# Pair products of a second set moved behind a stage of the chain on TensorE, and their inversion begun later

## The chip, the core and the metric

The kernel runs on one core of a Trainium2 chip. The metric is the device time of one execution, in microseconds; the time of a kernel is the median of its runs. A profile of one more execution shows where the time goes. The engines are TensorE (PE in the rows, PEld its weight loads), VectorE (DVE), ScalarE (ACT), GpSimd (POOL) and SyncE (SP), which issues most DMAs.

## The reference

A linear recurrence over 768 time steps for 4 x 8 heads, followed by a two-layer network on its outputs.

```python
for t in range(S):
    kt, vt, rt = (k[:, :, t], v[:, :, t], r[:, :, t])
    wt, at, bt = (w[:, :, t], a[:, :, t], b[:, :, t])
    y[:, :, t] = np.einsum('bhd,bhde->bhe', rt, state)
    Sa = np.einsum('bhde,bhe->bhd', state, at)
    state_decay = state * wt[:, :, None, :] - np.einsum('bhd,bhe->bhde', Sa, bt)
    state = state_decay + np.einsum('bhd,bhe->bhde', vt, kt)
...
h = x @ w_in
g = np.where(pos, h, np.where(neg, 0.0, (h + beta) ** 2 / (4.0 * beta)))
return (g @ w_out).astype(np.float32)
```

Here x is y laid out as 3072 tokens of 320, and w_in and w_out are 320 x 2048 and 2048 x 320.

## The kernel before

**Tiling.** The recurrence is cut into 24 chunks of 32 time steps; within a chunk it becomes small matmuls per head, with the inverse of a 32 x 32 triangular matrix for each head and chunk. Four chunks make a set (six sets). For a set the kernel needs the decayed rows of the inputs, the pair products of a and b (early_ab, line 208, for sets 0 and 1: 64 matmuls into one PSUM tile, line 217, copied to the tile `pairs` by ScalarE, line 221; called once for each half of the set), and the inversion (invert, line 361): `pairs` is turned on VectorE into `lw` (line 365), GpSimd sets the unit matrix (lines 367, 368), and then 31 pairs of products and subtractions follow (lines 376, 382), on VectorE for set 0 and on GpSimd for the others. adopt (line 385) turns the result into `tinv`.

**The chain** (line 517) runs a chunk in two halves of 16 heads, each in four stages: x0 (matmuls of line 532), the product with `tinv` (line 542, masks on VectorE at line 549, ScalarE copies at line 553), the state and the outputs (matmuls of lines 558 and 569, VectorE at 576 and 581), and the next state's product (lines 598, 600). The loop over chunks takes four steps for each chunk; each step runs one or two stages, loads and turns inputs (load_ti and load_cg; shift, line 323 on ScalarE; turn, lines 477, 480 and 482 on VectorE; scores, lines 498 and 510), and then calls fill. The first stage of chunk 0 is already run while set 0 is inverted; its second stage stands in the second step, its third in the third step.

**Fill** (line 928) hands out other work in six parts: columns of the two-layer network (feed; it begins only when two chunks of y have been laid out again, lines 618 to 627), one entry of the list `steps` (line 907), the conversion of the weights (wgen: ScalarE lines 764, 768 and 784, VectorE 772, GpSimd 785), and the background work (rows, ab and inv of later sets), whose pace is set by the table WINDOWS in chunks times ten: a window (a, b) for a set says when its work begins and when it must be done.

```python
            feed(1280)
            if first:
                first.pop(0)()
            due[0] += PACE
            while due[0] > 0:
                pull(wgen)
                due[0] -= 1
            background(now[0] + 10 / SLOTS * (k + 1) / 6)
```

Every engine works through its instructions in the order in which this program writes them.

Of the kernel before, what the change touches and what calls it, by code (L numbers as in the profile page):

```python
# [27 lines left out]
WINDOWS = dict(  # L28
    rows=[(0, 0), (24, 43), (46, 64), (70, 90), (106, 130)],
    ab=[(0, 0), (44.5, 55.5), (68, 84), (95, 119), (135, 159)],  # L30
    inv=[(2.1, 28), (56, 79.5), (85, 118), (121, 158), (161, 198)],
)

AHEAD = 5
# [21 lines left out]
def rwkv_moe_kernel(ctx: ExitStack, tc: tile.TileContext, r, k, v, w, a, b, w_in, w_out, ident_d, mask_d, out):  # L56
# [62 lines left out]
    def zero(x, row=0):  # L119
        z = zero_c[row : row + x.shape[0]]  # L120
        nc.scalar.copy(x, (z if len(x.shape) == 2 else z.unsqueeze(1)).broadcast_to(list(x.shape)))

    def init_cg(i, part):
        cg, pr = cgs[i], prs[i]
        if part == 0:
            return zero(cgf[i])
        if part == 2:
            return nc.gpsimd.memset(pr[:, :, :, 0:8], -1.0)
        for f in range(2):
            rows = slice(64 * f, 64 * f + D)  # L130
            nc.scalar.copy(
                cg[rows, f::2, C_G : C_G + D],
                ident[rows].unsqueeze(1).broadcast_to([D, 8, D]),
            )

    def copy_rv(s, part, c, n=1):

        x, o = ((r, O_R), (v, O_V))[part]
        nc.sync.dma_start(
            scr[s][0 : NH * 128].rearrange("(h x) e -> h x e", x=128)[:, L * c : L * (c + n), o : o + D],  # L140
            x.rearrange("b h t e -> (b h) t e")[:, 128 * s + L * c : 128 * s + L * (c + n), :],
        )
# [65 lines left out]
    def early_ab(s, half):  # L208

        ps = psum()  # L210
        for c in (2 * half, 2 * half + 1):
            for h in range(NH):
                p, f = h // 2, h % 2
                q, n = 2 * f + p % 2, 4 * p + c
                rows = slice(64 * f, 64 * f + D)
                at = 256 * (c % 2) + 32 * (p // 2)
                nc.tensor.matmul(
                    ps[32 * q : 32 * q + 32, at : at + 32],
                    lhsT=turned[s][0][rows, n, :], rhs=turned[s][1][rows, n, :], start=True, stop=True,
                )  # L220
        nc.scalar.copy(pairs_f[:, 512 * half : 512 * half + 512], ps)

    def early_store(s, c):

        nc.sync.dma_start(scr4[s][c, :, :, 80:240], early_out[s][c::4])
# [668 lines left out]
    i = 0  # L894
# [9 lines left out]
    owed, idle = [0], [True]  # L904
    now = [0]
    due = [0]
    steps = [[lambda half=half: early_ab(1, half)] for half in range(2)] + [[lambda: init_cg(2, 2)]] + [[lambda i=i, c=c: copy_rv(0, i, c)] for c in (2, 3) for i in range(2)]
    steps += [[] for _ in range(7)] + [[lambda c=c: early_store(1, c)] for c in range(4)] + [[] for _ in range(8)]
    steps += [[lambda i=i: copy_rv(1, i, 0, 4)] for i in range(2)]
    first = [lambda x=x: [f() for f in x] for x in steps]  # L910

# [118 lines left out]
```

## Time and profile before

| | |
|---|---|
| median of 3 runs | 779.89 us (777.26 to 780.51) |
| the profiled execution | 778.53 us, its span 776.8 us |
| TensorE busy, mean granted clock | 672.8 us (87%), 0.916 |
| VectorE, ScalarE, GpSimd busy | 589.2, 472.4, 433.2 us |
| HBM read, written | 70.88 MB, 27.53 MB |

Times in the rows count from the span's start. A timeline row gives start, duration, engine, line, operation, tiles and shape, and in brackets the idle time of the engine before it and what ended that. "issue" is idle time in which the engine waited for nothing that the profile shows. A matmul in float32 is shown as two records, so the 64 matmuls of one early_ab are 128 records. The granted clock is a share of the full 2.4 GHz; 0.50 is 1.2 GHz.

### The profile page before, as it was taken

To read this page: it belongs to the slowest core of one execution; us is meant where nothing else is said; L and a number is where in the kernel's file an instruction comes from. 1 tells how busy PE (TensorE), PEld (TensorE's weight loads), DVE (VectorE), ACT (ScalarE), POOL (GpSimd) and SP (SyncE) were. 2 spreads that over 40 slices of the span, in tenths; PEclk is the share of its full clock that TensorE was granted. 3 is DMA by queue.
4 is the path that set the end of the run, shared out by engine and by line. 5 is a ranking of instruction groups with operands and counts; after the bars stand their busy time and mean duration, and the time that the engine had idled before them with its cause. 6 is when DMAs were issued, how large, how long until landed. Compare 5 with 4: busy or idle time off the path is not lost.

```text
span 776.8 us, 35626 instructions
## 1 busy us (share of the span) xinstructions
PE 672.8 (87%) x15360; PEld 620.9 (80%) x15360; DVE 589.2 (76%) x1361; ACT 472.4 (61%) x1016; POOL 433.2 (56%) x603
## 2 busy tenths in 40 slices
PE   4546656796889889899988999999999999999997
PEld 4445546685779778789988889999999999999997
DVE  6999998887769678897788977788777786776211
ACT  5646756775566565565666566665665665655544
POOL 1232999765336998367576486563666732322332
PEclk9865656999699999999999999999999999999999
DMA  8898996998587758684558683443424234330100
GB/s 296 210 218 174 229 204 171 221 211 182 123 183 161 171 133 172 144 191 89 124 115 173 143 171 71 109 80 62 116 47 110 54 71 108 55 89 20 36 20 18
DMA packets 207084, 102.35 MB, mean 132 GB/s; under 512 B 153688, under 2 KB 200792, under 8 KB 206928
## 3 DMA queue, kind: packets, MB, share of 16 engines
q1 hardware_dynamic: 204336, 93.36, 54.2%
q0 software_dynamic: 2432, 6.56, 3.7%
q8 instruction: 121, 1.98, 1.1%
q14 instruction: 35, 0.29, 0.1%
q10 hardware_dynamic: 160, 0.16, 0.1%
HBM read 70.88 MB, written 27.53 MB: 127 GB/s over the span
## 4 chain that ended last, share of the span: by engine, by line
PE 54%; DVE 6%; POOL 4%; DMA 3%; ACT 2%; issue 2%; SPq 2%; POOLq 0%; ACTq 0%; DVEq 0%
PE ph L650 18%; PE po L681 17%; PE p L569 4%; PE p L558 3%; PE p L598 3%; PE p L498 2%; PE p L542 2%; PE p L532 2%; PE p L349 1%; DMA X<-Y 1%; POOL lw L382 1%; POOL lw L376 1%; POOL gl L667 1%; DVE gt L663 1%; DVE wz L235 1%
## 5 line engine op out<-in xcount | busy, mean ns | idle before, releaser
L650 PE MATMUL ph<-X,w 120*128 120x256 f32 x1536 | 219.7, 296 | 6.3 <-DMA X<-Y 5.8
L667 POOL TENSOR_TENSOR gl<-gt,gh 128x512 fp32r<-128x512 f32 x95 | 121.6, 1280 | 162.3 <-ACT gh L666 155.8
L650 PEld LDWEIGHTS ph<-X,w 120*128 120x128 f32 x1536 | 198.0, 198 | 13.9 <-issue 6.0
L681 PE MATMUL po<-w,gh 128*128 128x320 f32 x768 | 136.6, 320 | 4.6 <-ACT gh L666 3.8
L663 DVE SCALAR_TENSOR_TENSOR gt<-gt,ph 128x512 f32<-128x512 f32 x95 | 65.0, 684 | 85.2 <-ACT gt L661 72.8
L681 PEld LDWEIGHTS po<-w,gh 128*128 128x128 f32 x768 | 119.5, 197 | 6.7 <-ACT gh L666 5.0
L666 ACT CAST gh<-gt 128x512 fp32r<-128x512 f32 x95 | 58.8, 619 | 91.7 <-DVE gt L663 84.8
L660 ACT ACTIVATE gt<-ph,half_c 128x512 f32<-128x512 f32 x95 | 65.3, 687 | 54.5 <-PE ph L650 53.7
L382 POOL TENSOR_TENSOR lw<-lw 128x31 f32<-128x31 f32 (+15 forms) x155 | 86.9, 561 | 8.3
L376 POOL TENSOR_TENSOR lw<-lw 128x31 f32<-128x31 f32 (+15 forms) x155 | 85.5, 551 | 8.1
L576 DVE SCALAR_TENSOR_TENSOR cg<-p,pr 40x160 f32<-40x160 f32 x184 | 59.2, 322 | 34.6 <-PE p L569 32.5
L681 PE MATMUL po<-w,gl 128*128 128x320 f32 x384 | 75.8, 320 | 9.5 <-POOL gl L667 9.5
L510 DVE TENSOR_TENSOR cg<-p,mask 32x256 f32<-32x256 f32 x192 | 80.6, 420 | 3.6
L553 ACT ACTIVATE cg<-p 32x160 f32<-32x160 f32 x192 | 56.6, 295 | 30.6 <-DVE cg L549 16.3
L681 PEld LDWEIGHTS po<-w,gl 128*128 128x128 f32 x384 | 62.3, 195 | 11.6 <-POOL gl L667 11.3
L569 PE MATMUL p<-cg 128*64 128x72 f32 (+1 forms) x1536 | 64.0, 241 | 0.0
L549 DVE SCALAR_TENSOR_TENSOR cg<-p,mask 32x128 f32<-32x128 f32 x192 | 55.3, 288 | 11.0 <-ACT cg L553 5.8
L589 POOL TENSOR_TENSOR Y<-yt,Y 128x256 fp32r<-128x256 f32 x48 | 35.7, 744 | 48.5 <-ACT Y L588 48.4
L661 ACT ACTIVATE gt<-gt 128x512 f32<-128x512 f32 x95 | 60.0, 632 | 3.0
L569 PEld LDWEIGHTS p<-cg 128*64 128x64 f32 x1536 | 58.4, 150 | 0.4 <-issue 0.4
L558 PEld LDWEIGHTS p<-cg 128*40 128x40 f32 x1472 | 36.4, 131 | 21.2 <-ACT cg L553 13.1
L558 PE MATMUL p<-cg 128*40 128x40 f32 x1472 | 42.6, 219 | 12.2 <-ACT cg L553 12.2
(105 smaller groups left out, 1085.1 us busy)
## 6 DMA issues: line engine op xcount, KB each, us to landing
ti<-scr SPq DMA_DIRECT2D x96, 200.0 KB
cg<-scr SPq DMA_DIRECT2D x96, 80.0 KB
scr<-arena SPq DMA_DIRECT2D x16, 480.0 KB
X<-Y SPq DMA_DIRECT2D x36, 160.0 KB
scr<-wide SPq DMA_DIRECT2D x8, 640.0 KB
w<-in_moe_w_out_dram SPq DMA_DIRECT2D x16, 320.0 KB
tiab<-scr SPq DMA_DIRECT2D x28, 160.0 KB
cg<-scr SPq DMA_DIRECT2D x96, 40.0 KB
```

The source lines that it names most:

```text
L376: eng.tensor_mul(t3, W3[:, 0:n, j : j + 1].broadcast_to([128, n, m]), L3[:, j + 1 :, j].unsqueeze(1).broadcast_to([128, n, m]),)
L382: eng.tensor_sub(W3[:, 0:n, j + 1 :], W3[:, 0:n, j + 1 :], t3)
L510: nc.vector.tensor_tensor(out=cg[q, f::2, C_X : C_X + 64][:, 4 * i : 4 * i + 4].rearrange("p h (j x) -> p h j x", x=32), in0=ps[quarter(f, ...
L558: nc.tensor.matmul(pst[er[h % 2], h // 2, :], lhsT=cg[:, h, C_S : C_S + D], rhs=cg[:, h, C_G : C_G + D], start=True, stop=True)
L569: nc.tensor.matmul(psv[h // 8][64 * f : 64 * f + 64, h // 2 % 4, 0:n3], lhsT=cgw[:, h * CW + C_G : h * CW + C_G + 64], rhs=cg[:, h, C_R : ...
L576: nc.vector.scalar_tensor_tensor(out=cn[er[f], f::2, C_S : C_S + D][:, halves[i]], in0=psv[i][er[f], :, 32:72], scalar=-1.0, in1=pr[er[f], ...
L650: nc.tensor.matmul(phs[k % 2][:, n * j : n * j + n], lhsT=wt[0, f // 4, wi // 2][:, wi % 2, fs], rhs=Xs[g][:, xi, :], start=i == 0, stop=i ...
L660: nc.scalar.activation(gt, ph, AF.Relu, bias=half_c, scale=0.5)
L661: nc.scalar.activation(gt, gt, AF.Square)
L663: nc.vector.scalar_tensor_tensor(out=gt, in0=gt, scalar=1.0, in1=ph, op0=ALU.min, op1=ALU.max)
L667: nc.gpsimd.tensor_sub(gl, gt, gh.bitcast(F32))
L681: nc.tensor.matmul(pos[i], lhsT=x[:, ts_], rhs=w, start=q == 0 and k == 0, stop=end)
```

## The change

Two things. In the list `steps`, of which each fill hands out six entries, the two halves of early_ab for set 1 move from the first two places (first step) to places 6 and 7 (the first two parts of the second step's fill, which stand behind the second stage of the chain). What stood behind them moves up by two places: the clearing of `pr2`, the four copies of r and v for chunks 2 and 3, the four stores of set 1 and its two copies of r and v. And the window of set 1's inversion begins at 3.4 and not at 2.1; its end stays at 28.

```diff
-    inv=[(2.1, 28), (56, 79.5), (85, 118), (121, 158), (161, 198)],
+    inv=[(3.4, 28), (56, 79.5), (85, 118), (121, 158), (161, 198)],
...
-    steps = [[lambda half=half: early_ab(1, half)] for half in range(2)] + [[lambda: init_cg(2, 2)]] + [[lambda i=i, c=c: copy_rv(0, i, c)] for c in (2, 3) for i in range(2)]
-    steps += [[] for _ in range(7)] + [[lambda c=c: early_store(1, c)] for c in range(4)] + [[] for _ in range(8)]
+    steps = [[lambda: init_cg(2, 2)]] + [[lambda i=i, c=c: copy_rv(0, i, c)] for c in (2, 3) for i in range(2)]
+    steps += [[]] + [[lambda half=half: early_ab(1, half)] for half in range(2)] + [[] for _ in range(4)] + [[lambda c=c: early_store(1, c)] for c in range(4)] + [[] for _ in range(8)]
```

TensorE around the second stage of the chain's first half chunk, before (p are PSUM tiles, cg_85 the operands of chunk 0's first half, wide_104 the turned a and b of set 1):

```order
L532 MATMUL p_759<-cg_85 32x72 x16
L217 MATMUL p_819<-wide_104 32x32 x64
L217 MATMUL p_887<-wide_104 32x32 x64
L542 MATMUL p_963<-x_760,tinv 32x72 x2
...
L498 MATMUL p_991<-cg_86,ev 32x32 x16
L498 MATMUL p_991<-pr_89,ev 32x32 x16
L558 MATMUL p_1045<-cg_85 40x40 x16
```

and now:

```order
L532 MATMUL p_759<-cg_85 32x72 x16
L542 MATMUL p_829<-x_760,tinv 32x72 x2
...
L498 MATMUL p_857<-cg_86,ev 32x32 x16
L498 MATMUL p_857<-pr_89,ev 32x32 x16
L217 MATMUL p_901<-wide_104 32x32 x64
L217 MATMUL p_968<-wide_104 32x32 x64
L558 MATMUL p_1045<-cg_85 40x40 x16
```

The 128 matmuls of line 217 moved from ahead of the second stage (L542, eight rows in all) to between the scores (L498) and the third stage (L558).

VectorE at the same place (ti_82 are the next chunk's inputs, X the weights in conversion, cg_87 the next chunk's operands):

```order
 L772 SCALAR_TENSOR_TENSOR X_93<-X_93 120x512
-L365 STREAM_TRANSPOSE lw<-pairs 128x1024
-L549 SCALAR_TENSOR_TENSOR cg_85<-p_963,mask 32x4x32 x2
-L549 SCALAR_TENSOR_TENSOR cg_85<-p_964,mask 32x4x32 x2
-L510 TENSOR_TENSOR cg_86<-p_991,mask 32x4x64 x4
+L549 SCALAR_TENSOR_TENSOR cg_85<-p_829,mask 32x4x32 x2
+L549 SCALAR_TENSOR_TENSOR cg_85<-p_830,mask 32x4x32 x2
+L510 TENSOR_TENSOR cg_86<-p_857,mask 32x4x64 x4
 L482 STREAM_TRANSPOSE pr_90<-ti_82 128x16x32
 L772 SCALAR_TENSOR_TENSOR X_92<-X_92 120x512
+L365 STREAM_TRANSPOSE lw<-pairs 128x1024
 L772 SCALAR_TENSOR_TENSOR X_93<-X_93 80x512
```

The turn of the pairs (L365) moved from ahead of the masks (L549) to between two steps of the weights' conversion, behind L482 and ahead of L576.

GpSimd where the inversion of set 1 begins (w are converted weights):

```order
+L785 ISA
+L785 TENSOR_TENSOR w_00_1036<-X_93,w_00_1036 120x512
 L367 MEMSET lw 128x1024
 L368 MEMSET lw 128x32
-L785 ISA
-L785 TENSOR_TENSOR w_00_1039<-X_93,w_00_1039 120x512
-L785 TENSOR_TENSOR w_01_1113<-X_92,w_01_1113 120x512
+L785 TENSOR_TENSOR w_01_1114<-X_92,w_01_1114 120x512
+L785 TENSOR_TENSOR w_02_1123<-X_93,w_02_1123 80x512
+L790 DMA w_02_1123<-w_02_1123 40x512 x2
 L376 TENSOR_TENSOR lw<-lw 128x31
 L382 TENSOR_TENSOR lw<-lw 128x31
```

The first product of the inversion (L376) stands behind the third weight tile (w_02) and not behind the second. On ScalarE the two copies of line 221 move behind the shift of the next chunk's inputs (L323) and stand ahead of the weights' next L764.

## Rows read from the trace of the kernel before

**Rows 1.** Table of stretches: window, its length, busy us, clock, DMA share, GB/s.

```profile
52.00:60.00 8.00, 2.43 (x135) 1.99 (x136) 7.21 (x24) 0.40 (x1) 3.29 (x7) 0.50 0.99 231
60.00:67.00 7.00, 4.33 (x233) 3.80 (x232) 6.91 (x10) 4.16 (x8) 1.11 (x2) 0.50 0.49 130
67.00:80.00 13.00, 8.70 (x236) 7.67 (x237) 11.67 (x28) 9.18 (x21) 5.88 (x8) 0.50 1.06 215
80.00:125.00 45.00, 27.06 (x804) 24.07 (x804) 39.51 (x88) 30.80 (x72) 42.53 (x60) 0.65 1.01 202
...
450.00:730.00 280.00, 279.98 (x6376) 261.98 (x6375) 205.56 (x494) 172.79 (x380) 139.52 (x192) 1.00 0.36 79
```

In rows 1 the five busy times are those of PE, PEld, DVE, ACT and POOL, each with its count of instructions.

**Rows 2.** Timeline of TensorE (first row: its weight loads), 52 to 131 us.

```profile
52.11 0.25 PEld L532 LDWEIGHTS p<-cg 128*32 128x32 f32 x8 [0.26 <-issue]
...
52.56 1.82 PE L217 MATMUL p<-wide 40*32 40x32 f32 x119
59.95 1.93 PE L217 MATMUL p<-wide 40*32 40x32 f32 x128 [5.57 <-issue]
63.40 0.34 PE L217 MATMUL p<-wide 40*32 40x32 f32 x9 [1.52 <-issue]
63.67 1.18 PE L542 MATMUL p<-x,tinv 32*32 32x72 f32 x32
64.78 0.65 PE L498 MATMUL p<-cg,ev 40*32 40x32 f32 x32
65.23 0.63 PE L498 MATMUL p<-pr,ev 40*32 40x32 f32 x32
67.58 1.54 PE L558 MATMUL p<-cg 128*40 128x40 f32 x31 [1.73 <-ACT cg L553]
...
68.99 2.16 PE L569 MATMUL p<-cg 128*64 128x72 f32 x31
...
130.14 1.20 PE L650 MATMUL ph<-X,w 120*128 120x256 f32 x4 [2.69 <-DMA X<-Y]
```

**Rows 3.** DMA queues of the whole span: packets, MB, share of 16 engines.

```profile
q8 instruction: 121, 1.98, 1.1%
```

**Rows 4.** Timeline of VectorE, 60 to 74 us.

```profile
60.10 2.01 DVE L389 STREAM_TRANSPOSE tinv<-lw 128x1024 f32<-128x1024 f32 x1
...
63.46 0.71 DVE L480 STREAM_TRANSPOSE ev<-ti 128x512 f32<-128x512 f32 x1
...
64.67 1.94 DVE L365 STREAM_TRANSPOSE lw<-pairs 128x1024 f32<-128x1024 f32 x1
...
70.51 0.71 DVE L482 STREAM_TRANSPOSE pr<-ti 128x512 f32<-128x512 f32 x1 [0.91 <-ACT ti L323]
71.14 1.34 DVE L772 SCALAR_TENSOR_TENSOR X<-X 120x512 uint32<-120x512 uint32 x2
72.51 1.33 DVE L576 SCALAR_TENSOR_TENSOR cg<-p,pr 40x160 f32<-40x160 f32 x4
```

**Rows 5.** Timeline of ScalarE, 63 to 71 us.

```profile
63.80 0.58 ACT L221 COPY pairs<-p 128x512 f32<-128x512 f32 x1 [1.58 <-PE p L217]
...
70.02 0.45 ACT L323 COPY ti<-ti 32x320 f32<-32x320 f32 x1 [0.39 <-DMA ti<-scr]
```

**Rows 6.** Waits of SP's DMA queue, 40 to 130 us: total, times, longest.

```profile
SPq L317 <- DMA scr<-in_r_dram: 10.9, 1, 10.9
```

**Rows 7.** Timeline of GpSimd, 75 to 80 us.

```profile
75.15 1.28 POOL L785 TENSOR_TENSOR w<-X,w 120x512 fp32r<-120x512 f32 x1 [1.53 <-ACT w L784]
76.39 0.68 POOL L376 TENSOR_TENSOR lw<-lw 128x31 f32<-128x31 f32 x1
...
78.43 1.26 POOL L785 TENSOR_TENSOR w<-X,w 80x512 fp32r<-80x512 f32 x1
```

**Rows 8.** Waits of all engines, 60 to 140 us: total, times, longest.

```profile
ACT X L764 <- POOL w L785: 5.8, 3, 3.5
...
DVE yt L581 <- POOL Y L589: 2.4, 2, 1.9
```

## Prediction

> **What bounds the kernel now.** I read the table of stretches first [rows 1]. From 450 to 730 us TensorE is busy 279.98 of 280 us at the full clock, so whatever reaches it late there ends late by as much, one for one. The change lies far ahead of that, between 52 and 125 us. There TensorE works 2.43 of 8 us (52 to 60) to 27.06 of 45 (80 to 125), at 0.50 to 0.65 of its clock; DVE is busy 6.91 of 7 us from 60 to 67 and 39.51 of 45 from 80 to 125, and POOL 42.53 of those 45. In that part the kernel is a chain of steps (four for each chunk of 32 time steps), and the wide matmuls do not begin before two chunks are through. A delay in a step there shifts all that follows, unless something had time in hand.
>
> Next the timelines around the step. TensorE [rows 2]: both groups of pair products (L217, 64 matmuls each, which the trace shows as 128 records) stand ahead of the chain's second stage (L542). TensorE halts inside them for 5.57 and 1.52 us with the reason "issue", that is, for no semaphore. The halts come after 119 records, after 128 more, and leave 9: it takes its instructions in batches. The instruction queue's row says the same: 121 packets with 1.98 MB, 16.4 KB each [rows 3]. A batch began at 52.11 (8 records of L532, then 119), the next at 59.95, the next at 63.40: **turn-round 7.84 us and 3.45 us**. Bursts of small matmuls (128 records in 1.93 us) run through a batch faster than the next one comes.
>
> DVE [rows 4]: the inverse of the first set is turned by 62.11 and `ev` by 64.17; then the turn of the pairs, L365, takes 1.94 us ahead of the chain's masks. After the masks DVE idles 0.91 us for ACT's L323, and L323 waited for the DMA into `ti` and ended at 70.47 [rows 5]. That load had been held on SP's queue by copies of `r` (10.9 us) [rows 6], which the change doesn't touch. So **70.47 is a gate set by DMA**: L482 and two L772 follow it back to back, and L576 begins at 72.51, where TensorE's L569, half done, would have let it begin earlier.
>
> **The change, part by part.** (a) Taking L217 and L365 from ahead of the second stage. L542 can begin at 62.2 (tinv) and not at 63.67, the masks at 64.8 (after `ev` and one L772, half of 1.34) and not at 66.6 (64.67 + 1.94): 1.5 and 1.9 us, which overlap to under 2 us. On the path this is worth nothing: DVE's next work still waits for the gate at 70.47. Its cover is that DMA; were it gone, the gain would be the 1.9 us.
>
> (b) L365 now stands behind the gate. DVE: L482 from 70.51 to 71.22, the first L772 (half of 1.34 us) to 71.9, L365 to 73.85, the second L772 to 74.5. L576 begins then, 2.0 us later than 72.51. This term needs nothing but DVE's own order: **+2.0 us**.
>
> (c) L217 now stands ahead of L558. After `ev` at 64.17 come 64 records of L498 (about 1.08 us, from 64.78 to 65.86 in the trace of before), so L217 begins near 65.3. The batch that begins at 52.11 now holds 8 + 32 + 64 records and 23 of L217; these are through at 65.6. The batch after it has long come (it is there at 59.95). The one after that comes one turn-round later: 65.6 + 3.45 = 69.05 at best, 73.4 at worst. I take the lower end, since DMA is at 0.49 from 60 to 67 us and was at 0.99 when it took 7.84. The 105 records of L217 left then need 1.6 us: L558 begins at 70.65, against 67.58. It gets 23 records on, and the next batch is due. For this second turn-round the trace gives 3.45 at one end and 5.3 at the other (63.40 to about 68.7, where L558 ran through without a halt); I take 4.3, as DMA is dense again: 73.35. What is left of L558 and L569 took 2.45 us (68.7 to 71.15): L569 ends at 75.8, **4.65 us late on TensorE**. Its two halves free the two halves of L576 at 74.7 and 75.8; L576 ends at 76.5 against 73.84.
>
> So (b) and (c) run side by side, and their sum on the path is not 2.0 + 4.65 but the later of the two at L576: **+2.65 us**. After it DVE has no idle time to give (11.67 of the 13 us from 67 to 80 are busy, and the 0.91 lie before), so the step ends that much later.
>
> Of the batches the Trainium skill ("Runtime: NRT & Kernel Launch", section "Instruction fetch mechanics") says that engines refill in 16 KiB blocks and that crossing a boundary is mostly hidden. The size agrees with the 16.4 KB a packet; the halts of 5.57 and 1.52 us are against the second half. By that rule (c) would vanish and the sum would be +2.0 us.
>
> (d) Pieces that move with it. ACT: the two L221 (0.58 us each) move behind L323, ahead of the weights' L764; ACT then waits for L217's end (70.65) and has the pairs ready at about 71.3, in time for L365 at 71.9. The two L764/L768 pairs that stood behind L221 begin earlier, into idle time: nothing. POOL [rows 7]: the two memsets go behind the first L785, into a gap of 1.53 us or so: nothing. The four small inversion products from 76.39 to the L785 at 78.43, some 2.0 us that ran in a gap, now come behind that L785 and its two DMA issues, where POOL is 95% busy. Against that, the pace begins later (window 3.4 instead of 2.1), and about three products fewer stand ahead of the next L785. ACT waits 5.8 us for POOL's L785 and DVE 2.4 us for its L589 in this part [rows 8], so POOL decides: I count its lag as +1.7 us at the third L785, 2.3 near 84 to 100 us and, as the products that were put off must be made good by the end of the window, 2.9 near 124 us (an estimate: counts of products in the order by 0.55 to 0.65 us). SP: one copy of `v` goes ahead of a `ti` load, under 1 us on its queue; that load is wanted a step later: nothing. The four stores and two copies of the second set are handed out two places earlier but stand in the same order on SP: nothing.
>
> (e) From 125 us on the order is the same again. Sum: **+2.65 from the step, +2.9 by way of POOL; I take +2.8**. On the profiled execution's own time that is 778.53 + 2.8 = 781.3. That execution lies 1.36 us under the median of the three runs, so the forecast is 779.89 + 2.8 = **782.7 us**.
>
> **The rivals.** *No halts:* the batches come in time, (c) is gone and (b) stays: +2.0, 781.9 us. For it: no halt is seen from 64 to 80 us. Against: there no two bursts follow each other. Chance 0.12.
>
> *Given back:* POOL, not the step, sets the pace from 80 to 125 us, and has 2 to 3 products fewer ahead of each L785; ACT's waits of 5.8 us shrink. 0 to +1.5 us, 779.9 to 781.4. Chance 0.18.
>
> *Slower:* instruction batches take as long as the 7.84 us that one took under full DMA (0.99), and from 67 to 80 us DMA is at 1.06. Place: the two batches in and behind L217. One long one: 73.4, then 77.7, L569 ends at 80.15 and L576 0.67 later at 80.8, +7.0, 786.9 us; both long, +10.6, 790.5 us. It decides from a sum of both turn-rounds of about 9 us on (my sum has 7.75). Chance 0.18.
>
> *Faster:* the load into `ti` comes earlier than 70.47, so that (a) counts, and TensorE, whose work now stands closer together, gets its full clock before 83 us (the rows of L558 and L569 at the half clock are 1.54 and 2.16 us). -1.9 and some -2 for two steps at a better clock: -4, 775.9 us. For it: the clock is at 0.50 all the way from 52 to 80 us [rows 1]. Against: nothing of the change reaches the copies that hold the load. Chance 0.12.
>
> **How the numbers follow.** The forecast has 0.40, with its unknowns (second turn-round 3.45 to 5.3, POOL's lag 1.7 to 3) at +1.5 to +4.5. The measurement can tell about 0.5%, 3.9 us: below 776.0 is faster, above 783.8 slower. Faster: 0.08, most of the fourth rival. Slower: all of the third, 0.18, and some 0.12 of the forecast's upper end, 0.30. The rest, 0.62, is the same. The range leaves out about 0.1 at each end: below it most of the faster case, above it the third rival with more than one long batch: 778.0 to 787.5 us.
>
> **What would show it.** In the profile of after: L542 at about 62.2; L558 at 70 to 71 after L217, with "issue" halts of 1 to 2 us inside L217 and inside L558; L323 still ending near 70.5; L365 at about 72 and L576 at about 74.5 to 75; POOL's third L785 near 80; the first L650, 130.14 before [rows 2], near 133. It is wrong if L323 ends earlier, if L558 begins before 69 (no halts), if L558 begins after 74 (long batches), or if L576 is late but the first L650 isn't (given back).

## The result, and the profile after

The changed kernel takes **783.49 us** (median of 7 runs, 781.56 to 788.54), the kernel before, in as many runs beside it, 777.91. The ratio is 1.0076, with a 95% interval of 1.0047 to 1.0104: 5.9 us more, between 3.7 and 8.1. The forecast was 782.7 us, and 2.8 more than before. The time lies in the stated range, 0.8 us from the forecast. That nearness is luck in part, because the runs of before had a lower median this time than the three shown ahead (777.91 for 779.89): the difference is twice the forecast's, and can be told from none.

| | before | after |
|---|---|---|
| median | 777.91 us | 783.49 us |
| profiled execution, its span | 778.53, 776.8 us | 783.03, 781.2 us |
| first wide matmul (L650) begins | 130.14 us | 137.58 us |
| TensorE busy, mean granted clock | 672.8 us, 0.916 | 673.2 us, 0.906 |

Almost the same work, then, begun later. The timeline of TensorE after, from the second stage (L542) to the third (L558, L569) and at the first wide matmul:

```profile
62.35 1.18 PE L542 MATMUL p<-x,tinv 32*32 32x72 f32 x32 [9.53 <-DVE tinv L389]
...
65.27 0.45 PE L217 MATMUL p<-wide 40*32 40x32 f32 x15
69.04 1.93 PE L217 MATMUL p<-wide 40*32 40x32 f32 x128 [3.32 <-issue]
72.89 1.70 PE L217 MATMUL p<-wide 40*32 40x32 f32 x106 [1.91 <-issue]
74.52 0.95 PE L558 MATMUL p<-cg 128*40 128x40 f32 x21
77.02 0.56 PE L558 MATMUL p<-cg 128*40 128x40 f32 x10 [1.55 <-issue]
...
77.45 2.16 PE L569 MATMUL p<-cg 128*64 128x72 f32 x31
...
137.58 1.83 PE L650 MATMUL ph<-X,w 120*128 120x256 f32 x7 [2.45 <-DMA X<-Y]
```

Against [rows 2]: L542 begins 1.3 us earlier, at once after the turn of the inverse, as forecast. Then the pair products (L217) run in three pieces with two halts between them, and a third halt falls inside L558. L558 begins at 74.52 and not at 67.58, and L569 ends at 79.6 and not at 71.15.

VectorE after, against [rows 4], and ScalarE's shift and second copy of the pairs, against [rows 5]:

```profile
75.24 1.98 DVE L365 STREAM_TRANSPOSE lw<-pairs 128x1024 f32<-128x1024 f32 x1 [6.09 <-ACT pairs L221]
...
78.91 1.39 DVE L576 SCALAR_TENSOR_TENSOR cg<-p,pr 40x160 f32<-40x160 f32 x4
```

```profile
67.30 0.45 ACT L323 COPY ti<-ti 32x320 f32<-32x320 f32 x1 [0.45 <-DMA ti<-scr]
...
74.63 0.58 ACT L221 COPY pairs<-p 128x512 f32<-128x512 f32 x1 [3.31 <-PE p L217]
```

VectorE stands idle for 6.09 us, with the turn of the pairs (L365) at the head of its queue and the next weights and L576 behind it; ScalarE stands idle 3.31 us at L221 for the same reason. L576 begins at 78.91, 6.4 us later than at 72.51. The table row of this stretch (length, busy us of PE, PEld, DVE, ACT and POOL with counts, clock, DMA share, GB/s) says the same: from 67 to 80 us VectorE does 6.72 us of work, where it did 11.67 [rows 1].

```profile
67.00:80.00 13.00, 7.50 (x314) 7.07 (x317) 6.72 (x10) 5.23 (x10) 2.32 (x3) 0.50 0.94 210
```

From there the lag is carried to the first L650, 7.44 us late. That is one execution. Two more profiles of the same program (below) have the first L650 at 134.0 and 133.5, so this table of where L558 begins, against before, comes ahead of the experiments. It is made from the timelines of TensorE; L558 stands once in each step.

| L558 of before at | 67.58 | 134.09 | 289.74 | 338.54 | 453.38 | 701.80 |
|---|---|---|---|---|---|---|
| before once more | +2.16 | +0.47 | -0.74 | -0.66 | -0.17 | -0.14 |
| after | +6.94 | +7.17 | +8.36 | +8.23 | +6.00 | +5.99 |
| after, second profile | +4.08 | +3.94 | +4.71 | +7.35 | +8.17 | +8.21 |
| after, third profile | +2.96 | +3.33 | +3.02 | +5.62 | +6.31 | +6.35 |

The second and third profile of after were taken on one chip (15), before once more on another (4); which chips the first profiles of before and after ran on isn't on record. So a part of these differences may be the chip's.

Two things make the 5.9 us. The step costs 3.3 to 7.2 us by 134 us, and from 454 us on nothing changes. Between 290 and 454 us an execution gains 2.4 us or loses up to 3.5, and the rows there differ in the granted clock. The same L349 on TensorE and the rows of the two stretches behind it, first in before and then in the second profile of after:

```profile
314.81 0.33 PE L349 MATMUL p<-ea 40*32 40x32 f32 x16 [1.89 <-DVE ea L338]
```

```profile
315.00:320.00 5.00, 4.54 (x104) 3.92 (x92) 4.45 (x11) 2.75 (x5) 2.29 (x3) 0.66 0.26 70
320.00:325.00 5.00, 5.00 (x132) 4.75 (x124) 3.97 (x11) 3.92 (x10) 3.04 (x4) 1.00 0.91 221
```

```profile
319.64 0.33 PE L349 MATMUL p<-ea 40*32 40x32 f32 x16 [3.39 <-DVE ea L338]
```

```profile
320.00:325.00 5.00, 4.57 (x76) 4.11 (x80) 4.22 (x11) 2.76 (x5) 2.47 (x3) 0.51 0.26 70
325.00:330.00 5.00, 5.00 (x132) 4.45 (x121) 3.96 (x10) 2.47 (x8) 2.60 (x3) 0.50 0.93 226
```

TensorE stood idle 3.39 us and not 1.89, and the clock was then at half (0.51, 0.50) for both stretches of 5 us, where before had 0.66 in one and 1.00 in the next; from L558 to L558 the step takes 22.09 us for 18.05. This is why the experiments are compared at the first L650, ahead of such dips, beside their medians.

### The profile page after: what moved, and what is told of

The parts are those of the page before. It is cut to its first block, busy times and chain, and to the rows that moved or that the text cites. A ratio compares the mean times of both kernels' runs of the same rounds, so it can differ in the third digit from the quotient of the medians.

```text
span 781.2 us, 35626 instructions
## 1 busy us (share of the span) xinstructions
PE 673.2 (86%) x15360; PEld 621.7 (80%) x15360; DVE 591.0 (76%) x1361; ACT 472.5 (60%) x1016; POOL 431.9 (55%) x603
## 4 chain that ended last, share of the span: by engine, by line
PE 54%; DVE 6%; POOL 3%; ACT 2%; DMA 2%; issue 2%; SPq 1%; ACTq 0%; POOLq 0%; DVEq 0%
PE ph L650 19%; PE po L681 17%; PE p L569 4%; PE p L558 3%; PE p L598 3%; PE p L498 3%; PE p L532 2%; PE p L542 2%; PE p L349 1%; DMA X<-Y 1%; POOL lw L382 1%; DVE wz L235 1%; DVE ld_w L235 1%; POOL lw L376 1%; DVE gt L663 1%
## 5 line engine op out<-in xcount | busy, mean ns | idle before, releaser
L650 PE MATMUL ph<-X,w 120*128 120x256 f32 x1536 | 218.8, 296 | 6.2 <-DMA X<-Y 5.8
L650 PEld LDWEIGHTS ph<-X,w 120*128 120x128 f32 x1536 | 197.7, 197 | 13.5 <-issue 5.5
L681 PE MATMUL po<-w,gh 128*128 128x320 f32 x768 | 135.0, 318 | 3.9 <-ACT gh L666 3.3
L376 POOL TENSOR_TENSOR lw<-lw 128x31 f32<-128x31 f32 (+15 forms) x155 | 84.7, 546 | 8.1
L576 DVE SCALAR_TENSOR_TENSOR cg<-p,pr 40x160 f32<-40x160 f32 x184 | 59.2, 322 | 34.1 <-PE p L569 32.0
L681 PE MATMUL po<-w,gl 128*128 128x320 f32 x384 | 75.2, 318 | 9.1 <-POOL gl L667 9.1
L569 PE MATMUL p<-cg 128*64 128x72 f32 (+1 forms) x1536 | 65.8, 245 | 0.0
L549 DVE SCALAR_TENSOR_TENSOR cg<-p,mask 32x128 f32<-32x128 f32 x192 | 55.3, 288 | 11.0 <-ACT cg L553 5.9
L569 PEld LDWEIGHTS p<-cg 128*64 128x64 f32 x1536 | 60.1, 153 | 0.4 <-issue 0.4
L558 PE MATMUL p<-cg 128*40 128x40 f32 x1472 | 42.8, 219 | 13.4 <-ACT cg L553 11.8
L558 PEld LDWEIGHTS p<-cg 128*40 128x40 f32 x1472 | 36.6, 132 | 22.2 <-ACT cg L553 12.3
```

The source lines that it names most:

```text
L376: eng.tensor_mul(t3, W3[:, 0:n, j : j + 1].broadcast_to([128, n, m]), L3[:, j + 1 :, j].unsqueeze(1).broadcast_to([128, n, m]),)
L558: nc.tensor.matmul(pst[er[h % 2], h // 2, :], lhsT=cg[:, h, C_S : C_S + D], rhs=cg[:, h, C_G : C_G + D], start=True, stop=True)
L569: nc.tensor.matmul(psv[h // 8][64 * f : 64 * f + 64, h // 2 % 4, 0:n3], lhsT=cgw[:, h * CW + C_G : h * CW + C_G + 64], rhs=cg[:, h, C_R : ...
L576: nc.vector.scalar_tensor_tensor(out=cn[er[f], f::2, C_S : C_S + D][:, halves[i]], in0=psv[i][er[f], :, 32:72], scalar=-1.0, in1=pr[er[f], ...
L650: nc.tensor.matmul(phs[k % 2][:, n * j : n * j + n], lhsT=wt[0, f // 4, wi // 2][:, wi % 2, fs], rhs=Xs[g][:, xi, :], start=i == 0, stop=i ...
L681: nc.tensor.matmul(pos[i], lhsT=x[:, ts_], rhs=w, start=q == 0 and k == 0, stop=end)
```

## The experiments

Theory A: the loss is the batches in which TensorE takes its instructions. Each time a burst of small matmuls runs through a batch it waits for the next, and the change puts that wait in front of the third stage. Theory B: the loss is VectorE's order (L365 ahead of L576) and the products that GpSimd puts off. All kernels ran with a profile. The median of before beside them was 779.48 us for win34, few_after, few_before and double, and 778.93 for again_before, split12, place3 and early34. The last four (again_after_a to again_split12) were one run each, beside one run of before that took 783.0 us, so their times decide nothing, and they are read at their places in the trace.

| kernel | median, us | ratio to before (95%) | first L650, us | against 130.14 |
|---|---|---|---|---|
| after | 783.49 | 1.0076 (1.0047 to 1.0104) | 137.58 | +7.4 |
| win34 | 779.13 | 1.0008 (0.9975 to 1.0040) | 128.34 | -1.8 |
| few_after | 782.92 | 1.0031 (1.0000 to 1.0062) | 132.19 | +2.1 |
| few_before | 778.36 | 0.9987 (0.9953 to 1.0020) | 130.23 | +0.1 |
| double | 793.08 | 1.0164 (1.0121 to 1.0207) | 143.62 | +13.5 |
| again_before | 776.87 (one run) | | 130.55 | +0.4 |
| split12 | 781.88 | 1.0027 (1.0003 to 1.0052) | 133.77 | +3.6 |
| place3 | 787.60 | 1.0093 (1.0063 to 1.0124) | 136.36 | +6.2 |
| early34 | 779.57 | 1.0019 (0.9987 to 1.0052) | 129.62 | -0.5 |
| again_after_a | 785.26 (one run) | | 134.0 | +3.9 |
| again_after_b | 783.38 (one run) | | 133.5 | +3.3 |
| again_double | 797.91 (one run) | | 147.6 | +17.5 |
| again_split12 | 781.20 (one run) | | 132.8 | +2.6 |

**The window alone (win34).**

```diff
 # on the kernel before
-    inv=[(2.1, 28), (56, 79.5), (85, 118), (121, 158), (161, 198)],
+    inv=[(3.4, 28), (56, 79.5), (85, 118), (121, 158), (161, 198)],
```

> The kernel before with one part of the change alone: the inversion of set 1 begins at 3.4 and not at 2.1; its pair products stay where they were. Theory A (the change costs what TensorE's instruction batches cost, in front of the third stage L558): L558 begins at 65.5 to 67.6 us as before, L365 goes behind the masks, the time stays within 1.5 us of before (776.5 to 779.5). Theory B (the cost is the turn of the pairs, L365, on VectorE ahead of L576, and the inversion products put off on GpSimd): +2 to +4 us, 780 to 782, with L576 2 us later.

No difference in the median. VectorE in its timeline:

```profile
68.67 0.65 DVE L772 SCALAR_TENSOR_TENSOR X<-X 120x512 uint32<-120x512 uint32 x1
69.25 2.05 DVE L365 STREAM_TRANSPOSE lw<-pairs 128x1024 f32<-128x1024 f32 x1
...
71.90 1.33 DVE L576 SCALAR_TENSOR_TENSOR cg<-p,pr 40x160 f32<-40x160 f32 x4
```

L365 stands behind the gate here, as in the changed kernel, and L576 is still not late (71.90, before 72.51): the load into `ti` came early in this execution, L323 ended at 68.00 and not at 70.47, and the masks had gone first. GpSimd has the changed kernel's order here too, with the products put off, and the chain is 1.8 us early at the first L650. So neither the late beginning of the inversion nor GpSimd's order costs anything that shows in this execution; the interval of the median still leaves room for 3 us.

**Few records (few_after, few_before).** One matmul fills the whole PSUM tile in place of the 64 of a half, so the values of set 1's pairs are others and the rest is as it was.

```diff
 # in early_ab, on the changed kernel and on the kernel before
+        if s:
+            x, y = (turned[s][i][0:D].rearrange("p n t -> p (n t)") for i in range(2))
+            nc.tensor.matmul(ps, lhsT=x[:, 0:128], rhs=y[:, 0:512], start=True, stop=True)
-        for c in (2 * half, 2 * half + 1):
+        for c in () if s else (2 * half, 2 * half + 1):
```

> The changed kernel with the 64 pair matmuls of each half of set 1 replaced by one matmul that fills the same PSUM tile (the pairs of set 1 are then not the right ones; everything else stays). Theory A: with 4 records in place of 256 no batch halt is left ahead of L558; L558 begins at 65.5 to 67.5 us and not at 74.5, and the time falls from 783.5 to 776 to 780. Theory B: L558 begins early, but L576 still waits for L365 and GpSimd is still late, so 780 to 782 us.

The lag at the first L650 falls from 7.4 to 2.1 us, so 5.4 of the 7.4 of that profile go with the records (1.3 and 1.8 of the 3.3 and 3.9 of the other two). The lines of this kernel are higher by 3 (L561 is L558, L368 is L365, L579 is L576):

```profile
65.71 3.78 PE L213 MATMUL p<-wide 40*128 40x512 f32 x4
69.42 1.29 PE L561 MATMUL p<-cg 128*40 128x40 f32 x32
```

```profile
70.06 0.71 DVE L485 STREAM_TRANSPOSE pr<-ti 128x512 f32<-128x512 f32 x1 [1.94 <-ACT ti L326]
...
73.20 1.60 DVE L775 SCALAR_TENSOR_TENSOR X<-X 80x512 uint32<-80x512 uint32 x1
74.84 1.33 DVE L579 SCALAR_TENSOR_TENSOR cg<-p,pr 40x160 f32<-40x160 f32 x4
```

No halt is left. The replacement isn't free (its four records take 3.78 us), so L558 begins at 69.42 and not by 67.5, as theory A had it; but L569 is through by 72.7, and it is VectorE that L576 waits for. Here the load came late (70.02), and behind it stand L482, L772, L365 and L772: L576 begins at 74.84, **2.3 us later than before, which is term (b)** by its mechanism. Its size is larger than the prediction's: from the gate to L576 it takes 4.8 us (70.02 to 74.84) where it took 2.0 before (70.47 to 72.51), so 2.8 more and not 2.0. The second L772 took 1.60 us here and not half of 1.34. The median is above theory A's bound (782.92 against 776 to 780). In the profile L558 of this kernel is late by 2.04 us at 290 us and by 4.99 at 339: it has a dip of the clock there that before has not, like the second profile of after.

> The kernel before with the same replacement (one matmul for each half of set 1, which are then not the right pairs). Theory A: L542 begins right after the turn of the inverse at 62.2 and not at 63.7; L576 is still held by the load into ti, so the time is within 1 us of before, 776.9 to 778.9. If the first step's halts cost time (the fourth case of the prediction): 774 to 776 us.

Within 0.1 us at the first L650, and no difference in the median. VectorE and TensorE in its timelines:

```profile
72.29 1.33 DVE L579 SCALAR_TENSOR_TENSOR cg<-p,pr 40x160 f32<-40x160 f32 x4
```

```profile
62.77 1.18 PE L545 MATMUL p<-x,tinv 32*32 32x72 f32 x32 [6.09 <-DVE tinv L392]
```

The second stage starts at 62.77 without its halts, and L576 begins at 72.29 for 72.51: in the kernel before, the halts cost nothing, because they lie in the wait for the inverse and, behind it, VectorE and the load hold the step. This is what term (a) said.

**The records doubled (double).**

```diff
 # in early_ab, on the changed kernel
-        for c in (2 * half, 2 * half + 1):
+        for c in (2 * half, 2 * half + 1) * (1 + s):
```

> The changed kernel with every pair matmul of set 1 issued twice, 512 records in place of 256. Theory A: two more batches of 128 instructions pairs at 3.8 us each ahead of L558: L558 begins at about 82 us and not at 74.5, and the time goes from 783.5 to 789.5 to 792. Theory B': if only the records' own work counted (1.93 us for 128), L558 at 78.4 and 786.5 to 788.

```profile
65.46 2.16 PE L217 MATMUL p<-wide 40*32 40x32 f32 x143
70.09 1.93 PE L217 MATMUL p<-wide 40*32 40x32 f32 x128 [2.48 <-issue]
...
79.57 0.95 PE L558 MATMUL p<-cg 128*40 128x40 f32 x21
```

256 records more, and the first L650 is 6.0 us later than in the changed kernel. By the ratio the time is 12.8 us over its before (the change: 5.9), so some 7 us for two batches, whose work alone is 3.9 us; the intervals leave about 4 us either way, and the timeline is the surer sign: the batches of L217 begin 3.85 and 4.0 us apart (70.09, 73.94, 77.94). But L558 comes at 79.57, not 82: 143 records ran on without a halt from 65.46. The batch behind the first 23 records had come while TensorE waited for the inverse, as the prediction assumed of the changed kernel, and as it had not in the profile of after (69.04). This was what the last four runs were for.

**One half back (split12).**

```diff
 # on the changed kernel
-    steps = [[lambda: init_cg(2, 2)]] + ...
+    steps = [[lambda: early_ab(1, 0)]] + [[lambda: init_cg(2, 2)]] + ...
-    steps += [[]] + [[lambda half=half: early_ab(1, half)] for half in range(2)] + [[] for _ in range(4)] + ...
+    steps += [[lambda: early_ab(1, 1)]] + [[] for _ in range(5)] + ...
```

> The changed kernel with the first half of set 1's pair products back in the first step (ahead of L542) and the second half alone in the second step (ahead of L558). Theory A (turn-rounds of instruction batches in front of L558): 128 records fewer stand there, so only one halt is left, inside L558 (at about 69.4 us); L558 begins near 67.3, pairs are ready by 68, L576 begins at 72 to 74.5, and 776.5 to 781.5 us. Theory C (each half costs alike): half of the loss, L558 at 71, and 782 us or more with L365 behind the gate.

```profile
65.44 0.45 PE L217 MATMUL p<-wide 40*32 40x32 f32 x15
69.48 1.65 PE L217 MATMUL p<-wide 40*32 40x32 f32 x106 [3.59 <-issue]
...
73.99 0.56 PE L558 MATMUL p<-cg 128*40 128x40 f32 x10 [1.97 <-issue]
```

L558 comes at 71.07 and the lag at the first L650 is 3.6 us, half of that in the first profile of after: theory C by these two numbers, though the third profile of the changed kernel itself has 3.3; the median, 781.88, lies between the ranges of the two theories. I had assumed the batch after the first half to be loaded while TensorE waited 3.32 us for the inverse; it came only 4.0 us after the first records of the second half had begun their last run. Two batches begin behind `ev` and ahead of L576 here (69.48, 73.99), three in the changed kernel (69.04, 72.89, 77.02).

**One step later (place3).**

```diff
 # on the changed kernel
-    inv=[(3.4, 28), ...
+    inv=[(5.9, 28), ...
-    steps += [[]] + [[lambda half=half: early_ab(1, half)] for half in range(2)] + [[] for _ in range(4)] + [[lambda c=c: early_store(1, c)] for c in range(4)] + ...
+    steps += [[] for _ in range(7)] + [[lambda c=c: [early_store(1, c), early_ab(1, c) if c < 2 else None]] for c in range(4)] + ...
```

> The changed kernel with the pair products of set 1 one step later still, behind the third stage (L569, L532) and ahead of L598; the inversion's window begins at 5.9. Theory A: the burst costs its two to three turn-rounds of 3.8 us in front of whatever stands behind it: L598 begins at 81 to 82 us and not at 74.2, L600 waits for L365, and the time is +6 to +8, 784 to 787 us. Theory D (only the place in front of L558 is dear, since VectorE has work for this time in the third step): +0 to +3, 778 to 782.

```profile
72.95 2.66 PE L217 MATMUL p<-wide 40*32 40x32 f32 x179 [2.50 <-ACT ss L563]
78.02 1.28 PE L217 MATMUL p<-wide 40*32 40x32 f32 x77 [2.41 <-issue]
```

```profile
79.97 1.96 DVE L365 STREAM_TRANSPOSE lw<-pairs 128x1024 f32<-128x1024 f32 x1 [4.75 <-ACT pairs L221]
...
83.39 0.85 DVE L600 SCALAR_TENSOR_TENSOR cg<-p,pr 40x256 f32<-40x256 f32 x2
```

L558 is early (66.45) and L598 late by 5 us (79.23; theory A had 81 to 82, with a halt more); L600 waits behind L365, 5.9 us later than at 77.54. The first L650 is 6.2 us late, and the time is 7.2 us over its before by the ratio. Theory D falls and A holds in the main: the place in front of L558 isn't dear in itself, the one behind the third stage costs as much.

**In the dead time (early34).**

```diff
 # on the kernel before, with the window at 3.4
+    at(16, lambda: early_ab(1, 0))
+    at(24, lambda: early_ab(1, 1))
-    steps = [[lambda half=half: early_ab(1, half)] for half in range(2)] + [[lambda: init_cg(2, 2)]] + ...
+    steps = [[], []] + [[lambda: init_cg(2, 2)]] + ...
```

> The pair products of set 1 handed out while set 0 is still inverted (ahead of L532, where TensorE waits in any case), window at 3.4. Theory A: the halts fall into time in which TensorE has nothing to do before the inverse is turned at 62.3; L542 begins then, L558 at 65.5 to 66.5 us, and the time is that of before or up to 2 us less: 775.5 to 779. If halts reach L532 and through it L542: L542 at 63 to 65 and no gain, 778 to 781.

```profile
63.08 0.52 PE L532 MATMUL p<-cg 128*32 128x72 f32 x9 [4.73 <-issue]
64.08 1.18 PE L542 MATMUL p<-x,tinv 32*32 32x72 f32 x32 [0.49 <-ACT x L536]
```

The halts reach L532, and L542 begins at 64.08: the second case of the expectation. No difference to before, and nothing won.

**Before once more (again_before).** The same program, for its gate.

> The kernel before once more, for a second profile of it. The load into ti that L323 waits for ended at 70.47 us in the first profile and between 68.0 and 70.3 in those of five other kernels, whose programs are the same up to there. If that end varies by execution, it will lie elsewhere than 70.47 here (67.5 to 70.5), and L576 (72.51) will move with it by less than 1 us, as L365 stands ahead of the masks; if it is fixed by the program, 70.3 to 70.6.

```profile
60.67 1.93 PE L217 MATMUL p<-wide 40*32 40x32 f32 x128 [5.85 <-issue]
65.77 0.34 PE L217 MATMUL p<-wide 40*32 40x32 f32 x9 [3.17 <-issue]
```

```profile
70.21 1.00 ACT L323 COPY ti<-ti 32x320 f32<-32x320 f32 x2 [0.21 <-DMA ti<-scr]
```

L323 ended at 71.21, outside even the range that I gave (which left out a profile, too: the lowest of the five other kernels was the changed one's, 67.75 and not 68.0). So the gate lies elsewhere in each execution, 67.53 to 71.29 us in fourteen profiles, though no program here differs ahead of it in what moves data. The turn-round between 60.67 and 65.77 was 5.10 us and not 3.45. In all, this execution is 0.4 us later at the first L650.

**Is the batch loaded in the wait (again_after_a, again_after_b, again_double, again_split12).** Four of the kernels above once more, unchanged.

> The changed kernel once more, for one question: the batch of instructions behind the first 23 records of L217 came at 69.04 us, 3.77 after them (65.27), and was not loaded in the 9.53 us in which TensorE had waited for the inverse. Theory E: whether it is loaded in that wait is set by the program; then L217 halts here too behind its first records, goes on near 69 (68.5 to 69.8), L558 begins at 74 to 75.3 and the first L650 near 137 to 138. Theory F: it varies with the execution; then in one look or the other 151 records run on without a halt from about 65.3, L558 begins at 70.5 to 72, and the first L650 lies near 133 to 134.

> The same program a third time, with the same numbers: a halt behind the first 23 records until about 69 and L558 at 74 to 75.3 by theory E, 151 records without a halt and L558 at 70.5 to 72 in some look by theory F.

> The kernel with the records doubled once more. There the batch was there: 143 records ran on without a halt from 65.46, and the next came at 70.09. Theory E: the same again, L558 near 79.6 and the first L650 near 143.6. Theory F: in some look it halts behind the first 23 records until about 69 and comes to L558 one batch later, at 83 to 84, first L650 near 147.

> One half ahead of the second stage, once more. There the second half's first records ran at 65.44 and the next batch came at 69.48. Theory E: the same, L558 near 71.1 and the first L650 near 133.8. Theory F: in some look the second half runs on without a halt, L558 begins at 67.5 to 68 and the first L650 is near 130 to 131.

TensorE and VectorE in again_after_b, the third profile of the changed kernel:

```profile
65.20 2.16 PE L217 MATMUL p<-wide 40*32 40x32 f32 x143
68.91 1.70 PE L217 MATMUL p<-wide 40*32 40x32 f32 x106 [1.55 <-issue]
70.54 0.95 PE L558 MATMUL p<-cg 128*40 128x40 f32 x21
73.59 0.56 PE L558 MATMUL p<-cg 128*40 128x40 f32 x10 [2.09 <-issue]
...
74.01 2.16 PE L569 MATMUL p<-cg 128*64 128x72 f32 x31
```

```profile
71.60 1.96 DVE L365 STREAM_TRANSPOSE lw<-pairs 128x1024 f32<-128x1024 f32 x1
73.48 1.66 DVE L772 SCALAR_TENSOR_TENSOR X<-X 80x512 uint32<-80x512 uint32 x1
75.25 0.66 DVE L576 SCALAR_TENSOR_TENSOR cg<-p,pr 40x160 f32<-40x160 f32 x2
76.21 0.66 DVE L576 SCALAR_TENSOR_TENSOR cg<-p,pr 40x160 f32<-40x160 f32 x2 [0.30 <-PE p L569]
```

Theory F, it varies with the execution. Here 143 records run on without a halt, and there are two halts on the path and not three. In again_after_a, the second profile, the batch came 0.39 us late, at 65.91, and the next at 70.03; L558 began at 71.66. The doubled kernel went the other way:

```profile
65.34 0.45 PE L217 MATMUL p<-wide 40*32 40x32 f32 x15
69.12 1.93 PE L217 MATMUL p<-wide 40*32 40x32 f32 x128 [3.32 <-issue]
...
84.80 0.95 PE L558 MATMUL p<-cg 128*40 128x40 f32 x21
```

It halts where it had not, for the 3.32 us of the first profile of after, and its first L650 moves from 143.62 to 147.6, by one turn-round, about as theory F had it (83 to 84 and 147; measured 84.80 and 147.6; at L558 it is 5.2 us, because a later turn-round took 5.4 us here). The same program, then, with and without that halt, 4.0 us apart. again_split12 didn't show what theory F allowed it: it halted again, for 2.22 us (its next piece of L217 began at 68.06, 1.4 us earlier than in split12).

The trace also shows where the batch was meanwhile. The instruction queue q8 moved 121 packets of 16.4 KB [rows 3], and TensorE's profile has 15360 matmul and as many weight-load records: 254 to a packet, a batch. Each batch of L217 in these five profiles of the changed and the doubled kernel begins 1.3 to 1.5 us after a packet of q8 has ended. From 51 to 66 us, in the wait for the inverse and the first 23 records, q8 has one packet in again_after_b and one in double (from 55.89 and 56.65 us), one in again_after_a (from 63.44), and none in after and again_double, where the next begins at 66.25 and 66.74. The row of q8 in again_after_b for 51 to 66 us (packets, MB, share of 16 engines), and the row of after for 62 to 64 us:

```profile
q8 instruction: 1, 0.02, 0.6%
```

```profile
62.00:64.00 2.00, 1.18 (x32) 0.94 (x32) 1.97 (x5) 0.38 (x2) 0.00 (x0) 0.50 0.05 10
```

So in the first profile the batch wasn't slow on its way: its transfer began only when TensorE had run dry, although the DMA share from 62 to 64 us was 0.05. The two repeats of the changed kernel ran on one chip, and their packets still lie 7.55 us apart (55.89 and 63.44), so the chip alone doesn't decide it.

## Why the prediction was right or wrong, point by point

**What bounds the kernel: right.** A delay of the step goes through to the first wide matmul whole (in the first profile 6.5 us at the end of L576 and 7.44 at L650, in the third 3.0 and 3.3), and from 456 to 741 us TensorE is busy 284.98 of 285 us after, as it was before (279.98 of 280).

**(a), the work taken from ahead of the second stage is worth nothing: right.** few_before shows it with the halts gone. The reason given, a fixed gate at 70.47, was too simple: the gate moves by 3.8 us from one execution to the next.

**(b), +2.0 us for L365 behind the gate: right in its mechanism where the gate is late, its size 0.8 us too small.** In few_after and in the third profile of after (gate at 70.36, VectorE free for L576 at 75.2) it is 4.8 us from the gate to L576 for 4.0 in the sum, because the second L772 took 1.60 and 1.66 us. Where the gate is early (win34) the term is nothing. In the third profile TensorE is later still, as the forecast had it: the second half of L576 waits for L569 at 76.21.

**(c), the batches: the mechanism is right, and so is the sum, on a premise that fails in some executions.** In the third profile of after the sum's own times came out one by one: the batch inside L217 at 68.91 (forecast 69.05), L558 at 70.54 (70.65), the batch inside L558 at 73.59 (73.35), L569 through at 76.2 (75.8), L576 through at 76.9 (76.5), the first L650 at 133.5 (near 133). The +2.65 of the sum measured 3.0. The step that failed is the sentence "The batch after it has long come (it is there at 59.95)". In the kernel before, TensorE stood halted, out of instructions, until 59.95, and the packet came within that halt (57.19 to 58.50). After the change TensorE stands at that time in its wait for the inverse with records in hand, and whether the next batch is fetched meanwhile isn't certain. In the first profile it wasn't, and came only at 69.04, 3.77 us after the last run of the first 23 records; by then 233 records of L217 were left and not 105, and three turn-rounds lay on the path. By the prediction's own durations that gives 69.05, 73.35, L558 at 74.9 (74.52 measured), 77.65, L569 through at 80.1 (79.6) and L576 through at 80.8, 7.0 us late (80.3, 6.5 late). The batch at 69.04 is not the one that the forecast has at 69.05 but the one ahead of it; the times agree because both come one turn-round behind the first 23 records.

So the term is 3.0 to 3.9 us or 6.5 to 7.4, by the execution (at the end of L576 and at the first L650), where I had put 2.65 alone.

**(d), GpSimd: not a term of its own.** It was to be 1.7 us late at its third L785, and is late by 1.56 and 2.14 in the third and second profile (79.99 and 80.57 against 78.43), by 4.99 in the first. But win34 has the same order there without the step's delay and loses nothing, -1.61 us at the first L558 and -1.78 at 134 us; and in the third profile of after the step's 3.0 us alone account for the 3.3 at 134. The counts of products were right; that they decide was not.

**(e), no difference from 125 us on: right for the order, wrong for the time of one execution.** The dips of the clock between 290 and 454 us move it by -2.4 to +3.5 us. The change's executions ended, at the last L558, 5.99, 8.21 and 6.35 us late. That the two with the smaller step lost 3.3 and 3.5 us there and the one with the larger gained 2.4 may be chance or may hang on how late each comes. Of the twelve profiles of kernels other than before, eight lose 2.2 to 3.3 us between 290 and 339 us, win34 and few_after among them; again_before and before itself have no such loss. What sets it is open, and with it some 1.5 us of the 5.9 (the three profiles of after are on average 5.4 us late at 290 us and 6.9 at 702).

**The rivals.** *Slower* came true by its sign, and in one execution by its size (+7.0 forecast, +6.5 at L576), but not by its mechanism: no turn-round there took 7.84 us, there was one more of them. *No halts* falls: there were two or three. Crossing from one batch to the next cost 3.32, 1.91 and 1.55 us in the first profile of after and 1.55 and 2.09 in the third, since 128 records take 1.93 us and a batch 3.5 to 4.7. Of the batches the Trainium skill says ("Runtime: NRT & Kernel Launch", section "Instruction fetch mechanics") that crossing a boundary is mostly hidden. These halts are against it, for bursts as small as these. *Given back* did not happen ahead of 290 us. *Faster* falls with the gate: it did come early in the first profile of after (67.75), and VectorE then waited for the pairs.

**The chances.** 0.62 for no measurable difference rested on +2.8 with one count of halts. By the prediction's limits the time (783.49, under 783.8) is the same, which had 0.62, but the difference (5.9, over 3.9 us) is slower, which had 0.30. With the batch's coming as an unknown of the sum, between 2.65 and 7.0, the forecast would have stood near +4.8, and most of the chance at slower.

## What to carry to other kernels

Many small matmuls cost more than their own time, namely their instructions' time: 128 records of 15 ns ran in 1.93 us (granted clock 0.50), and the next batch came 3.5 to 5.4 us after the one before had begun, once 7.84. Put such a burst where the engine waits in any case; between two stages of this chain each batch showed up in the time, at both places tried. And where a trace shows that something was there when it was asked for, don't take it to be there unasked: carry both cases into the range.

## What the hardware showed that I hadn't expected

A batch of instructions may or may not be fetched while an engine waits for a semaphore: with the same program the next 128 records ran on at once (65.20 in the third profile of after, 65.46 in double), came 0.39 us late, or came 3.32 us after the engine had run dry (69.04 in the first profile, 69.12 in again_double). The packets of the instruction queue show that the transfer itself began late, up to 10.8 us later than in the earliest of the five profiles (55.89 to 66.74); what decides when it begins the runs don't show. A load's landing, with the same program ahead of it, moved from 67.53 to 71.29 us over fourteen profiles. And in one step an idle time of TensorE of 3.39 us for 1.89 came with a granted clock of 0.51 and 0.50 in the 10 us behind it, for 0.66 and 1.00, and the step was 4.0 us longer.
